# Another way to normalise the last attention block: reciprocals on the queries' partitions, four columns a tile

## Chip, cores and metric

One core of one Trainium2 chip. The time is device microseconds of one execution of the whole program; a kernel's figure is the median over several runs. The core has five engines that run their own instruction queues in order: TensorE (PE, matrix products, with weight loads listed as PEld), VectorE (DVE), ScalarE (ACT), GpSimd (POOL) and SyncE (SP, which here only issues transfers).

## What is computed

A transformer block over 2048 rows of 448 columns: layer norm, then attention with 16 heads of 28 columns, and, from the same normalised rows, a gate made by a feed-forward network. The output is the input plus attention times gate.

```python
x = A_x                                   # [1, 2048, 448], bfloat16
xn = _layernorm(x)
qkv = xn @ wqkv                           # 16 heads, 28 columns each
p = softmax(q @ k.T * 28 ** -0.5)
s = (p @ v) @ wo
g = silu(gelu(xn @ w1 + b1) @ w2 + b2)
return x + s * g
```

## The kernel before

The 16 heads lie in four groups (`G`) of four, each head padded to 32 partitions, and the 2048 queries in four chunks (`C`) of 512. A block is one group and one chunk, so there are 16 blocks. For each block the scores of 16 tiles of keys are computed in four row tiles of TensorE (line 1210), most are exponentiated on ScalarE two or three banks at a time (line 1266), some in pieces on VectorE (lines 1366 and 1417 to 1424), and the product with the values (P·V, line 1478) collects in one PSUM bank, `acc`. The values carry a column of twos, so that a head's softmax sum lies in row 28 of its 32 rows.

The last block (group 3, chunk 3) is cut by queries: one piece of 256 queries (tiles 0 and 1) and two of 128 (tiles 2 and 3); `pieces` does this. When P·V of a piece is done, `p_epi4` copies it from `acc` to `E_sb` (line 1510) and runs `p_norm4` for each of its tiles. That spreads the sums over a head's 32 partitions by a 128x128 matmul with the constant `selb` (line 1521), inverts 128x128 values on VectorE (line 1524) and multiplies (line 1527) into `qT`, which here holds the normalised attention. The 15 blocks before it do it in another way, in `p_epi`: a matmul with the four columns of `sel` brings the sums onto the queries' partitions (line 1543), VectorE inverts 16 columns (line 1546), GpSimd splits the result into a high and a low bfloat16 part (lines 1548 and 1549), and small column-tiled matmuls spread it back (line 1558).

`p_last` then multiplies a tile of the last chunk with `wo` (line 1575; groups 0 to 2 first, group 3 when the tile is normalised), and `t_oev` multiplies by the gate (line 1584), adds the input (line 1586) and issues the output transfer on SyncE's queue (line 1590). `p_out` does the same for the chunks before, with two tiles to a transfer (line 1592). The gate of the last tile is made late, behind the last exponential: a tanh on ScalarE (line 1167) and two instructions on GpSimd (lines 1169 and 1171).

The order on every engine is not written out. A planner (`run`) holds many small processes; each offers its next task with a duration, a latency and a priority, and the planner keeps a clock for each engine. It takes the task that can start first and, among those of the same engine that can start within 0.1 us of it, the one with the lowest priority number. The engines then run this fixed order, each waiting on semaphores for what it needs. When TensorE would be idle, `p_busy` fills in matmuls with zeros (line 895), until the last exponentials. Two PSUM banks that no other process holds for good go from process to process (`K.banks`); after the last scores those of the scores are added.

At the start, GpSimd makes small constants (`selb` at line 568, `bsel4` at line 571) and then the squares of a part of the key weights (line 765), while VectorE normalises the first chunk (line 696).

The lines around which all turns are these two, of the planner and of the wait for the last tile's first matmuls:

```python
near = [c for c in cand if c[1][3].E == E and c[0] <= s0 + EPS]
bank, tok = yield ("bank", lambda: K.g_done[c] and (K.on4[t] or (pre and K.exp_m >= MTOT - 7)))
```

Of the kernel before, what the change touches and what calls it, by code (L numbers as in the profile page):

```python
# [7 lines left out]
ACTF = mybir.ActivationFunctionType  # L8
ALU = mybir.AluOpType
ET = mybir.EngineType  # L10

PE, ACT, DVE, POOL, SP = ET.PE, ET.Activation, ET.DVE, ET.Pool, ET.SP
# [7 lines left out]
C = 4  # L20
# [7 lines left out]
MTOT = NBLK * T * 4  # L28
# [45 lines left out]
class _Kernel:  # L74
# [21 lines left out]
    def sb(self, name, shape, dtype=dt.bfloat16):  # L96
        return self.es.enter_context(self.nc.sbuf_tensor(name, shape, dtype))
# [160 lines left out]
    def alloc(self):  # L258
        nc = self.nc
        f32, bf = dt.float32, dt.bfloat16  # L260
        sb = self.sb
        B = _Buf
# [32 lines left out]
        self.lnv = sb("lnv", [128, T], f32)  # L295
        self.rstd = sb("rstd", [128, T], f32)
        self.nm = sb("nm", [128, T], f32)
        self.selb = sb("selb", [128, 128], bf)
        self.rc = sb("rc", [128, 16], f32)
        self.rhi = sb("rhi", [128, 16], bf)  # L300
        self.rlo = sb("rlo", [128, 16], bf)
# [8 lines left out]
        self.g_sb = self.h[:, :, 0:1792].rearrange("p c (t d) -> p c t d", d=D)  # L310
        self.osb = self.h[:, :, 1792:3584].rearrange("p c (t d) -> p c t d", d=D)
        self.iota_f = self.h[:, 1, 0:256].bitcast(f32)
        self.rf = self.w1[:, 0, 0:512].bitcast(f32).rearrange("p (a b) -> p a b", a=2)
        self.wsq = self.h[:, 1, 512:2560].rearrange("p (k n) -> p k n", k=4)
        self.stg = self.h[:, 2, 0:KT * 2 * D].rearrange("p (k w h d) -> p k w h d", k=KT, w=2, d=DH)
        ps = lambda n, s: self.es.enter_context(nc.psum_tensor(n, s, f32))
# [49 lines left out]
        self.b_P += self.b_hf[2][5:14] + self.b_hf[3][0:12] + [B() for _ in range(16)]  # L366
        self.pon = [(0, NP)]
        self.b_nm = [[B(), B()] for _ in range(C)]
        self.b_selb = B()
        self.b_E4, self.b_on4, self.b_o4 = ([B() for _ in range(4)] for _ in range(3))  # L370
        self.b_rf = [B(), B()]
        self.b_sum, self.b_sum2, self.b_m3 = B(), B(), B()
        self.b_sig3, self.b_g3 = B(), B()
        self.banks = [(self.misc[:, :], self.b_misc), (self.acc[:, :], self.b_acc)]
# [8 lines left out]
    def schedule(self):  # L383
        K = self
# [16 lines left out]
        K.g_done = [False] * C  # L401
        K.on_done = [False] * NBLK
        K.on4 = [False] * 4
        K.ln_done = 0
        K.taken = 0
        K.next_m = 0
# [85 lines left out]
    def constants(self):  # L492
        K = self
        e = self.emit

        def f(eng):
# [15 lines left out]
          writes=[K.b_pads], dur=0.1)  # L512
# [26 lines left out]
        for thr in (32.0, 64.0, 96.0):  # L539
# [3 lines left out]
              reads=[ec, tc], writes=[ec], dur=0.3)  # L543

        def f(eng):
# [6 lines left out]
          reads=[K.b_cols], writes=[tc], dur=0.3)  # L552
# [11 lines left out]
        def f(eng):  # L564
            return eng.tensor_copy(K.sel[:, :], K.ident[:, :].rearrange("p (j e) -> p j e", e=32)[:, :, DH])
        e(POOL, f, reads=[K.b_id], writes=[K.b_bsel], dur=0.2)
        selb = K.selb[:, :].rearrange("p (j e) -> p j e", e=32)
        e(POOL, lambda eng: eng.tensor_copy(selb, K.sel[:, :, None].to_broadcast([128, 4, 32])), reads=[K.b_bsel],
          writes=[K.b_selb], dur=0.3)
        bs4 = K.bsel[:, :].rearrange("p (j e) -> p e j", e=32)[:, 24:32, :]  # L570
        e(POOL, lambda eng: eng.tensor_copy(K.bsel4[:, :].rearrange("p (e j) -> p e j", j=4), bs4), reads=[K.b_bsel],
          writes=[K.b_bsel4], dur=0.2)
# [933 lines left out]
    def p_epi4(self, s):  # L1506
        K = self
        ts = ((0, 1), (2,), (3,))[s]
        sl = slice(128 * ts[0], 128 * (ts[-1] + 1))
        yield _Task(DVE, lambda eng: eng.tensor_copy(K.E_sb[:, 1, sl], K.acc[:, sl]), [K.b_acc, K.b_E[1]],  # L1510
                    [K.b_E4[t] for t in ts], 0.16 + 0.13 * len(ts), 0.0, 0)
        K.E_done = NBLK - 1 + s
        for t in ts:
            yield from K.p_norm4(t)

    def p_norm4(self, t):
        K = self
        g, c = G - 1, C - 1
        E, tE = K.E_sb[:, 1, 128 * t:128 * (t + 1)], K.b_E4[t]
        bank, tok = yield ("bank", lambda: K.g_done[C - 1])  # L1520
        yield _Task(PE, lambda eng: eng.matmul(bank[:, 0:128], K.selb[:, :], E, start=True, stop=True),
                    [tE, K.b_selb], [tok], 0.1, 0.12, 3)
        R = K.rf[:, t % 2, :]
        yield _Task(DVE, lambda eng: eng.reciprocal(R, bank[:, 0:128]), [tok], [K.b_rf[t % 2]], 0.96, 0.0, 1)
        K.banks.append((bank, tok))
        dst = K.qT[:, g, c * 512 + 128 * t:c * 512 + 128 * (t + 1)]
        yield _Task(DVE, lambda eng: eng.tensor_tensor(dst, E, R, ALU.mult), [tE, K.b_rf[t % 2], K.b_qT[g][c]],
                    [K.b_on4[t]], 0.3, 0.0, 1)
        K.on4[t] = True

    def p_epi(self, b):
# [48 lines left out]
    def t_oev(self, ps, tok, c, t):  # L1580
        K = self
        o = K.osb[:, c, t, :]
        wr = K.b_osb[c][t // 2] if c < C - 1 else K.b_o4[t]
        yield _Task(DVE, lambda eng: eng.tensor_tensor(o, ps, K.g_sb[:, c, t, :], ALU.mult),
                    [tok, K.b_g3 if (c, t) == (C - 1, 3) else K.b_g[c]], [wr], 0.63, 0.0, 3)
        yield _Task(DVE, lambda eng: eng.tensor_tensor(o, o, K.x2[:, c, t, :], ALU.add),
                    [K.b_x2[c], wr], [wr], 0.4, 0.0, 3)
        ov = K.out[0].rearrange("(c p t) d -> c p t d", p=128, t=4)[c]
        if c == C - 1:
            K.outs.append(K.dma(SP, lambda eng: eng.dma_start(ov[:, t, :], o), K.s_out[6 + t], reads=[wr]))  # L1590
        elif t % 2:
            K.outs.append(K.dma(SP, lambda eng: eng.dma_start(ov[:, t - 1:t + 1, :], K.osb[:, c, t - 1:t + 1, :]),
                                K.s_out[2 * c + t // 2], reads=[wr]))
# [10 lines left out]
    def p_last(self, t):  # L1604
        K = self
        c = C - 1
        pre = t == 3
        bank, tok = yield ("bank", lambda: K.g_done[c] and (K.on4[t] or (pre and K.exp_m >= MTOT - 7)))
        ps = bank[:, 0:D]
        yield K.t_wo(ps, tok, c, t, (0, 1, 2), 3)  # L1610
        yield ("until", lambda: K.on4[t])
        yield K.t_wo(ps, tok, c, t, (3,), 3)
        yield from K.t_oev(ps, tok, c, t)
        K.banks.append((bank, tok))
# [51 lines left out]
```

## Time and profile before

| | us |
|---|---|
| median of 4 runs (464.2 to 464.68) | 464.52 |
| the profiled execution: its time | 464.2 |
| its span | 462.4 |
| ScalarE busy | 448.4 (97%) |
| TensorE busy | 440.0 (95%) |
| VectorE busy | 372.3 (81%) |
| GpSimd busy | 37.6 (8%) |
| ScalarE: first exponential starts | 12.57 |
| ScalarE: the tanh behind the last exponential starts | 454.87 |
| reciprocal of 128x128 (line 1524), 4 times, each | 0.94 to 0.96 |
| reciprocal of 128x16 (line 1546), 15 times, each | 0.25 to 0.26 |
| output transfers of the last chunk, issue to landing, median | 1.7 |

The span runs from the first to the last recorded instruction; the time of the same execution is 1.8 us longer. Lines of a timeline give start, duration, engine, line, operation, what is written and read, how many instructions were merged, and in brackets the idle time ahead and what ended it. An engine's busy share says which engine works most on average; what an edit is worth is read in the stretch where it stands.

### The profile page before, as it was taken

Reading aid. Unit: us, or ns where it says so; the run is one execution under the profiler, and the core shown is the slowest. Engines: PE = TensorE matmul, PEld = TensorE weight load, DVE = VectorE, ACT = ScalarE, POOL = GpSimd, SP = SyncE. Lnnn points to the kernel's source line nnn. Section 1 sums busy time; section 2 is a strip of 40 time slices with the busy share of each in tenths; the row PEclk is TensorE's granted clock in tenths of the full one; section 3 lists DMA queues with packets and bytes.
Section 4 is the critical chain, followed back from the end, with each engine's and each line's share of the span. In section 5 each row is a group of like instructions: output and inputs, shape, how many; then the busy total and the mean of one; then the engine's idle time right before and its main releaser. Section 6 shows DMA issues by size and latency. Waiting matters only on the chain.

```text
span 462.4 us, 10812 instructions
## 1 busy us (share of the span) xinstructions
PE 440.0 (95%) x4555; PEld 169.8 (37%) x4555; DVE 372.3 (81%) x588; ACT 448.4 (97%) x407; POOL 37.6 (8%) x79
## 2 busy tenths in 40 slices
PE   6999999999999999999999999999999999999995
PEld 4533333333323232323233343333333344343562
DVE  8956898898879797988888844889469698888796
ACT  6999999999999999999999999999999999999994
POOL 7480000001000000100000010000000001000001
PEclk9999999999999999999999999999999999999999
DMA  8401000000000000000040000101000010100001
GB/s 264 150 2 37 2 1 0 3 1 3 2 1 1 1 1 1 2 1 2 1 140 1 1 1 0 42 2 41 0 14 28 1 41 2 42 1 21 23 23 61
DMA packets 8385, 11.17 MB, mean 24 GB/s; under 512 B 1697, under 2 KB 6993, under 8 KB 8338
## 3 DMA queue, kind: packets, MB, share of 16 engines
q1 hardware_dynamic: 8050, 9.80, 6.9%
q8 instruction: 36, 0.59, 0.5%
q10 hardware_dynamic: 288, 0.69, 0.4%
q14 instruction: 11, 0.09, 0.1%
HBM read 8.61 MB, written 1.84 MB: 23 GB/s over the span
## 4 chain that ended last, share of the span: by engine, by line
PE 52%; ACT 35%; issue 9%; DVE 2%; DMA 1%; POOL 0%; ACTq 0%; DVEq 0%; POOLq 0%
ACT P L1266 17%; PE ring L1210 14%; ACT h L1266 11%; PE acc L1478 10%; PE ring L1079 6%; ACT xnT L1266 6%; PE misc L1138 5%; PE ring L1138 4%; PE acc L895 3%; PE misc L1079 2%; PE ring L734 2%; PE misc L734 2%; PE misc L1210 1%; PE ring L1575 1%; DMA x_sb<-in_A_x_dram 1%
## 5 line engine op out<-in xcount | busy, mean ns | idle before, releaser
L1266 ACT ACTIVATE P<-ring 128x1024 bf16<-128x1024 f32 (+1 forms) x194 | 222.1, 1258 | 1.8 <-PE ring L1210 0.9
L1210 PE MATMUL ring<-qT,kT 32*128 32x512 bf16 (+2 forms) x1088 | 143.7, 358 | 12.5 <-ACT P L1266 5.2
L1266 ACT ACTIVATE h<-ring 128x1024 bf16<-128x1024 f32 (+1 forms) x97 | 114.3, 1293 | 0.2
L1210 PEld LDWEIGHTS ring<-qT,kT 32*128 32x128 bf16 x1088 | 37.1, 91 | 132.7 <-ACT P L1266 53.6
L1266 ACT ACTIVATE xnT<-ring 128x1536 bf16<-128x1536 f32 (+1 forms) x72 | 83.5, 1284 | 0.2 <-PE misc L1210 0.2
L1478 PE MATMUL acc<-P,vaug 128*32 128x512 bf16 (+2 forms) x535 | 47.5, 358 | 0.0
L895 PE MATMUL acc<-ident,zero 128*128 128x128 bf16 x525 | 41.5, 220 | 0.0
L1079 PE MATMUL ring<-xnT,w 128*128 128x512 bf16 x160 | 41.1, 381 | 0.0
L1548 POOL CAST rhi<-rc 128x16 bf16<-128x16 f32 x15 | 6.6, 440 | 389.2 <-DVE rc L1546 344.3
L895 PEld LDWEIGHTS acc<-ident,zero 128*128 128x128 bf16 x525 | 29.7, 98 | 17.6 <-issue 16.7
L1138 PE MATMUL misc<-w,h 128*128 128x448 bf16 x126 | 30.1, 355 | 0.0
L1478 PE MATMUL acc<-h,vaug 128*32 128x512 bf16 x241 | 25.1, 384 | 0.0
L1210 PE MATMUL misc<-qT,kT 32*128 32x512 bf16 (+1 forms) x64 | 24.1, 379 | 0.0
L1138 PE MATMUL ring<-w,h 128*128 128x448 bf16 x98 | 22.3, 354 | 0.1
L1366 DVE TENSOR_SCALAR x_sb<-ring 128x512 uint16<-128x512 f32 x22 | 15.2, 689 | 7.6 <-PE ring L1210 7.2
L1536 DVE CAST E_sb<-acc 128x512 bf16<-128x512 f32 x15 | 10.4, 691 | 13.2 <-PE acc L1478 13.0
L1079 PEld LDWEIGHTS ring<-xnT,w 128*128 128x128 bf16 x160 | 12.8, 97 | 18.7 <-issue 5.2
L1079 PE MATMUL misc<-xnT,w 128*128 128x512 bf16 x64 | 18.3, 383 | 0.0
L1478 PE MATMUL acc<-xnT,vaug 128*32 128x512 bf16 (+2 forms) x240 | 18.2, 330 | 0.0
L1366 DVE TENSOR_SCALAR w<-ring 128x512 uint16<-128x512 f32 x20 | 13.7, 687 | 4.0 <-PE ring L1210 4.0
L1478 PEld LDWEIGHTS acc<-P,vaug 128*32 128x32 bf16 x535 | 11.9, 95 | 13.8 <-issue 10.2
L1117 ACT ACTIVATE h<-h 128x2560 bf16<-128x2560 bf16 (+2 forms) x8 | 16.6, 2072 | 0.0
(278 smaller groups left out, 658.3 us busy)
## 6 DMA issues: line engine op xcount, KB each, us to landing
h<-in_A_x_dram SPq DMA_DIRECT2D x4, 448.0 KB, 3.1
w<-in_B_w_dram SPq DMA_DIRECT2D x1, 1568.0 KB, 7.4
w<-in_B_w_dram SPq DMA_DIRECT2D x1, 1344.0 KB, 9.0
out_dram<-h SPq DMA_DIRECT2D x6, 224.0 KB, 1.9
x_sb<-in_A_x_dram SPq DMA_DIRECT2D x2, 448.0 KB, 5.1
h<-in_A_wqkv_dram SPq DMA_DIRECT2D x3, 168.0 KB, 5.0
x_sb<-in_A_x_dram ACTq DMA_DIRECT2D x1, 448.0 KB, 4.3
out_dram<-h SPq DMA_DIRECT2D x4, 112.0 KB, 1.7
```

The lines of the kernel that those rows point to most:

```text
L734: ins = eng.matmul(bank, w[:, kt, g * 128:(g + 1) * 128], K.xnT[:, kt, c * 512:(c + 1) * 512], start=(kt == 0), stop=(kt == KT - 1))
L895: ins = eng.matmul(K.acc[:, 0:128], K.zero[:, :], K.ident[:, :], start=False, stop=True, skip_group_check=True)
L1079: ins = eng.matmul(bank, K.w1[:, kt, ft * 128:(ft + 1) * 128], K.xnT[:, kt, c * 512:(c + 1) * 512], start=(kt == 0), stop=(kt == KT - 1))
L1117: yield _Task(ACT, lambda eng, dst=dst, src=src: eng.activation(dst, src, ACTF.Gelu_apprx_tanh), rd, K.b_hf[c][f0:f0 + n] + ([K.b_h[c]] if ...
L1138: ins = eng.matmul(ps, hv[:, ft, t * 128:(t + 1) * 128], K.w2[:, ft, :], start=(ft == 0), stop=(ft == FT - 1))
L1210: return eng.matmul(dst, K.kT[32 * j:32 * j + 32, g, t * 128:(t + 1) * 128], K.qT[32 * j:32 * j + 32, g, c * 512 + q0:c * 512 + q0 + nq], ...
L1266: return eng.activation(reg[:, i0:i0 + n, :], K.ring[:, b0:b0 + n, :], ACTF.Exp, scale=SM_SCALE)
L1366: yield _Task(DVE, lambda eng: eng.tensor_scalar(K.unit[u][:, 512 * k:512 * k + 512].bitcast(dt.uint16), bank, SM_SCALE * LOG2E * 128.0, ( ...
L1478: return eng.matmul(K.acc[32 * j:32 * j + 32, q0:q0 + nq], K.vaug[:, t, 4 * g + j, :], ap[:, col:col + nq], tile_position=(0, 32 * j), sta ...
L1536: yield _Task(DVE, lambda eng: eng.tensor_copy(E, K.acc[:, :]), [K.b_acc], [tE], 0.7, 0.0, 0)
L1548: yield _Task(POOL, lambda eng: eng.tensor_copy(K.rhi[:, :], K.rc[:, :]), [K.b_rc], [K.b_rhl], 1.1, 0.0, 1)
L1575: ins = eng.matmul(ps, K.qT[:, g, c * 512 + t * 128:c * 512 + (t + 1) * 128], K.wo[:, g, :], start=(g == 0), stop=(g == G - 1))
```

## The change

The last block's tiles are normalised as the other blocks are, one tile of 128 queries at a time: a matmul with the four columns of `sel`, a reciprocal of 128x4, the split into `rhi` and `rlo`, now on VectorE instead of GpSimd, eight column-tiled matmuls, and a multiplication straight out of PSUM. All of these have priority 0. The bank is held until the multiplication is queued. The constant `selb`, the buffer `rf` and their tokens are removed. The copy of the last piece (tile 3) is made on ScalarE. In `t_oev` the gate multiplication of the last tile gets priority 2 instead of 3, and the add 3.5, 3, 2.5 and 2 for tiles 0 to 3 instead of 3. In `p_last` the first three matmuls of the last tile are offered once the selection matmul of tile 3 is queued (`K.n4 == 3`), where they were offered when few exponentials were left.

```diff
-        selb = K.selb[:, :].rearrange("p (j e) -> p j e", e=32)
-        e(POOL, lambda eng: eng.tensor_copy(selb, K.sel[:, :, None].to_broadcast([128, 4, 32])), reads=[K.b_bsel],
-          writes=[K.b_selb], dur=0.3)
...
-        yield _Task(DVE, lambda eng: eng.tensor_copy(K.E_sb[:, 1, sl], K.acc[:, sl]), [K.b_acc, K.b_E[1]],
-                    [K.b_E4[t] for t in ts], 0.16 + 0.13 * len(ts), 0.0, 0)
+        E4 = K.E_sb[:, 1, sl]
+        if s == 2:
+            yield _Task(ACT, lambda eng: eng.activation(E4, K.acc[:, sl], ACTF.Copy), [K.b_acc, K.b_E[1]],
+                        [K.b_E4[t] for t in ts], 0.3, 0.0, 0)
+        else:
+            yield _Task(DVE, lambda eng: eng.tensor_copy(E4, K.acc[:, sl]), [K.b_acc, K.b_E[1]],
+                        [K.b_E4[t] for t in ts], 0.16 + 0.13 * len(ts), 0.0, 0)
...
-        yield _Task(PE, lambda eng: eng.matmul(bank[:, 0:128], K.selb[:, :], E, start=True, stop=True),
-                    [tE, K.b_selb], [tok], 0.1, 0.12, 3)
-        R = K.rf[:, t % 2, :]
-        yield _Task(DVE, lambda eng: eng.reciprocal(R, bank[:, 0:128]), [tok], [K.b_rf[t % 2]], 0.96, 0.0, 1)
+        yield _Task(PE, lambda eng: eng.matmul(bank[:, 128:132], E, K.sel[:, :], start=True, stop=True),
+                    [tE, K.b_bsel], [tok], 0.06, 0.17, 0)
+        K.n4 = t
+        rc, hi, lo = (x[:, 4 * t:4 * t + 4] for x in (K.rc, K.rhi, K.rlo))
+        t1, t2, t3 = _Buf(), _Buf(), _Buf()
+        yield _Task(DVE, lambda eng: eng.reciprocal(rc, bank[:, 128:132]), [tok, K.b_rhl], [t1], 0.15, 0.0, 0)
+        yield _Task(DVE, lambda eng: eng.tensor_copy(hi, rc), [t1, K.b_rhl], [t2], 0.07, 0.0, 0)
+        yield _Task(DVE, lambda eng: eng.tensor_tensor(lo, rc, hi, ALU.subtract), [t1, t2, K.b_rhl], [t3], 0.07, 0.0, 0)
+
+        def f(eng):
+            ins = None
+            for k, r in enumerate((hi, lo)):
+                for j in range(4):
+                    ins = eng.matmul(bank[32 * j:32 * j + 32, 0:128], r[:, j:j + 1].to_broadcast([128, 32]),
+                                     K.ident[:, :], tile_position=(0, 32 * j), start=(k == 0), stop=(k == 1),
+                                     skip_group_check=True)
+            return ins
+        yield _Task(PE, f, [t2, t3, K.b_id], [tok], 0.12, 0.17, 0, mode="col")
+        dst = K.qT[:, g, c * 512 + 128 * t:c * 512 + 128 * (t + 1)]
+        yield _Task(DVE, lambda eng: eng.tensor_tensor(dst, bank[:, 0:128], E, ALU.mult), [tE, tok, K.b_qT[g][c]],
+                    [K.b_on4[t]], 0.3, 0.0, 0)
         K.banks.append((bank, tok))
-        dst = K.qT[:, g, c * 512 + 128 * t:c * 512 + 128 * (t + 1)]
-        yield _Task(DVE, lambda eng: eng.tensor_tensor(dst, E, R, ALU.mult), [tE, K.b_rf[t % 2], K.b_qT[g][c]],
-                    [K.b_on4[t]], 0.3, 0.0, 1)
         K.on4[t] = True
...
-                    [tok, K.b_g3 if (c, t) == (C - 1, 3) else K.b_g[c]], [wr], 0.63, 0.0, 3)
+                    [tok, K.b_g3 if (c, t) == (C - 1, 3) else K.b_g[c]], [wr], 0.63, 0.0, 2 if (c, t) == (C - 1, 3) else 3)
...
-                    [K.b_x2[c], wr], [wr], 0.4, 0.0, 3)
+                    [K.b_x2[c], wr], [wr], 0.4, 0.0, 3.5 - 0.5 * t)
...
-        bank, tok = yield ("bank", lambda: K.g_done[c] and (K.on4[t] or (pre and K.exp_m >= MTOT - 7)))
+        bank, tok = yield ("bank", lambda: K.g_done[c] and (K.on4[t] or (pre and K.n4 == 3)))
```

More of the change, by code (lines that the diff above doesn't have):

```diff
@@ L297, in alloc @@
         self.nm = sb("nm", [128, T], f32)
-        self.selb = sb("selb", [128, 128], bf)
         self.rc = sb("rc", [128, 16], f32)
@@ L312, in alloc @@
         self.iota_f = self.h[:, 1, 0:256].bitcast(f32)
-        self.rf = self.w1[:, 0, 0:512].bitcast(f32).rearrange("p (a b) -> p a b", a=2)
         self.wsq = self.h[:, 1, 512:2560].rearrange("p (k n) -> p k n", k=4)
@@ L368, in alloc @@
         self.b_nm = [[B(), B()] for _ in range(C)]
-        self.b_selb = B()
         self.b_E4, self.b_on4, self.b_o4 = ([B() for _ in range(4)] for _ in range(3))
-        self.b_rf = [B(), B()]
         self.b_sum, self.b_sum2, self.b_m3 = B(), B(), B()
@@ L403, in schedule @@
         K.on4 = [False] * 4
+        K.n4 = -1
         K.ln_done = 0
```

## The prediction

> **What bounds the kernel now.** I read the page's busy shares first (ScalarE is busy 97% of the span), then ScalarE's waits (2.2 us in all from its first exponential on), then the chain of waits, and last the timeline of the two stretches where ScalarE is not the bound: before its first exponential at 12.57 us and after its last one, behind which the tanh of line 1167 begins at 454.87 us. In between the exponentials run one after another, so the change can win only at the two ends, and can lose wherever it lets ScalarE wait. The timeline of the tail (start, duration, engine, line, operation):
>
> ```profile
> 454.87 0.69 ACT L1167 ACTIVATE w<-w 128x448 bf16<-128x448 bf16 x1
> ...
> 455.63 1.03 POOL L1169 TENSOR_TENSOR h<-w 128x448 bf16<-128x448 bf16 x1 [17.92 <-ACT w L1167]
> ...
> 455.92 0.29 DVE L1510 CAST E_sb<-acc 128x128 bf16<-128x128 f32 x1 [0.21 <-PE acc L1478]
> ...
> 456.13 0.78 DVE L1586 TENSOR_TENSOR h<-h 128x448 bf16<-128x448 bf16 x1
> ...
> 456.74 1.05 POOL L1171 TENSOR_TENSOR h<-h,w 128x448 bf16<-128x448 bf16 x1
> 456.83 0.61 DVE L1584 TENSOR_TENSOR h<-misc,h 128x448 bf16<-128x448 f32 x1
> 457.37 0.94 DVE L1524 RECIPROCAL w<-ring 128x128 f32<-128x128 f32 x1
> 458.41 0.29 DVE L1527 TENSOR_TENSOR qT<-E_sb,w 128x128 bf16<-128x128 bf16 x1
> ...
> 458.76 0.36 PE L1575 MATMUL ring<-wo,qT 128*128 128x448 bf16 x1 [1.97 <-DVE qT L1527]
> 459.16 0.62 DVE L1584 TENSOR_TENSOR h<-ring,h 128x448 bf16<-128x448 f32 x1 [0.16 <-PE ring L1575]
> 459.82 0.39 DVE L1586 TENSOR_TENSOR h<-h 128x448 bf16<-128x448 bf16 x1
> ```
>
> The reader is to see that from the end of the last copy (456.21) to the last gate multiplication (459.16) 2.95 us pass, all on VectorE's queue: an add and a multiplication of earlier tiles stand ahead of the reciprocal, and the reciprocal itself takes 0.94. From 459.16 on (multiplication, add, output transfer, span's end at 462.4) nothing is changed. Note also the add at 456.13: 0.78 us, while GpSimd runs.
>
> **Part 1, the tail.** New chain from 456.21 on. ScalarE's copy replaces VectorE's. No row has 128x128 out of PSUM on ScalarE; its 128x256 rows (line 860) take 0.38 and its 128x2 rows (line 679) 0.20, which bound it; half way in size is 0.29, VectorE's time, so I take 0, bounds -0.09 and +0.09. ScalarE's tanh is over at 455.56, nothing is queued behind the copy. Then:
> - to TensorE 0.06 (458.70 to 458.76 in the tail), the matmul with the four selection columns 0.26, to VectorE 0.04: reciprocal starts at 456.57. VectorE must be free then. Tiles 0 to 2 no longer pay 0.94 each, and have priority 0, so their multiplications and adds should be over by 455.5; that is where the 1.16 us from 456.21 to 457.37 goes.
> - reciprocal of 128x4: 128x16 takes 0.25, 128x128 0.945, that is 6.2 ns a column, so 0.17; gap 0.05: 456.79.
> - the copy to rhi and the subtraction to rlo, new on VectorE: its 128x1 rows (lines 656, 667) take 0.15 and 0.14, its 128x128 rows 0.29; near the small end, 0.15 and 0.17 with a gap of 0.05: done at 457.16.
> - eight column matmuls: the 32 of line 1558 occupy TensorE from 439.67 to 440.25, 0.018 each, the last takes 0.23; with two hops 0.06+0.15+0.23+0.05: 457.65. The three matmuls of tile 3 that now wait for n4 (0.73 us, 456.00 to 456.73 in the trace) run behind the selection matmul to about 457.2, under the VectorE chain.
> - multiplication out of PSUM 0.29 (line 1565: 0.69 for 512 columns), hop, matmul, hop 0.46: the gate multiplication starts at 458.40 instead of 459.16, **-0.76**.
>
> Now GpSimd. The two new small instructions read SBUF at 456.8 to 457.2, in the middle of line 1171. The trace shows what that can cost:
>
> ```profile
> L1586 DVE TENSOR_TENSOR h<-h x16: 380/392/777, 395.9 to 459.8; 128x448 bf16<-128x448 bf16 x16
> ```
>
> ```profile
> 6.03 0.67 DVE L696 TENSOR_SCALAR h<-x_sb,mv,rstd 128x448 bf16<-128x448 bf16 x2
> ...
> 6.85 0.29 POOL L568 COPY selb<-sel 128x128 bf16<-128x128 bf16 x1
> ...
> 7.08 0.23 POOL L571 COPY bsel<-bsel 128x32 bf16<-128x32 bf16 x1
> 7.28 0.93 POOL L765 TENSOR_TENSOR h<-h 128x448 bf16<-128x448 bf16 x1
> ...
> 7.60 1.04 DVE L696 TENSOR_SCALAR h<-x_sb,mv,rstd 128x448 bf16<-128x448 bf16 x2
> ```
>
> One add of sixteen is twice as long, the one that began 0.5 us into line 1169; it ended 0.25 us after GpSimd's instruction. The pair of line 696 takes 0.67 us at 6.03 and 1.04 at 7.60, beside line 765. So a VectorE instruction that reads SBUF behind a running two-input GpSimd instruction waits for its end. Line 1171 starts at 456.74 and takes 0.93 as line 765 does, to 457.67; the subtraction then ends at about 457.77, and the gate multiplication starts at 459.01: **-0.15**; if the copy to rhi is held as well, about 0. The two ends of this term are -0.85 (a faster ScalarE copy, no block) and 0; I take -0.15, because the nearest row, the add, was held by exactly this pair of instructions. The pair at 6.03 beside line 560 was not held, which keeps the other end alive.
>
> The Trainium skill (SBUF — State Buffer, section "Who interferes with whom") states that a VectorE instruction with two SBUF inputs contends with a GpSimd instruction that reads SBUF, and that whoever comes second blocks fully. The add at 456.13 agrees (0.78 against 0.39), and by this rule the tail is worth -0.15, without it -0.76.
>
> **Part 2, the head.** The copy that makes selb (line 568) goes. It is 0.23 us of GpSimd's queue (6.85 to 7.08), and line 765, which follows with no idle time, starts at 7.05 and ends 0.23 earlier. The held instruction at 7.60 took 0.74 where its neighbours take 0.37 to 0.39, so 0.36 of wait shrinks by 0.23. The chain of waits passes through it, then transposes, ScalarE's and VectorE's copies (ScalarE idled only 0.16 before the one at 9.21), qT and the first exponential at 12.57. Bounds -0.23 and 0 (another wait takes over); I take **-0.2**. On TensorE the column sums of line 915 may come a place earlier, 0.24 us, beside a wait.
>
> **Part 3, the middle of the last block.** Each of tiles 0 to 2 adds eight column matmuls (0.15 us) to TensorE's queue, ahead of which they wait for VectorE. Behind them stand P·V and scores. By the priorities, tile 0's group comes between the projection of the third block's last tile and P·V at 448.05:
>
> ```profile
> 448.05 0.63 PE L1478 MATMUL acc<-P,vaug 128*32 128x128 bf16 x32
> 448.61 0.40 PE L1210 MATMUL ring<-qT,kT 32*128 32x128 bf16 x12
> ```
>
> ```profile
> 449.06 2.44 ACT L1266 ACTIVATE xnT<-ring 128x1536 bf16<-128x1536 f32 x2
> ```
>
> The scores end at 449.01 and their exponential starts at 449.06: no slack. So whatever the group adds here ScalarE loses: 0.15, and up to 0.3 with a late rlo. The later scores have slack: the twelve at 450.67 feed an exponential at 451.30. Bounds 0 (dropped filler matmuls) and +0.3; I take **+0.2**.
>
> **At nothing.** The new priorities of the add (line 1586; its output transfer goes behind it on SyncE in the same order of tiles and with the same bytes): in blocks 12 to 14 each add follows its own multiplication with no other add ready; if two swap, 0.39 under 0.9 us of exponential. The bank held through the multiplication: two floating banks and, at the end, the returned score banks cover it; without them one projection, 0.7, off the path until 455. Removed buffers cost nothing.
>
> **Sum.** -0.15 - 0.2 + 0.2 = -0.15. The profiled execution took 464.2 (span 462.4 and 1.8 around it), the fastest of those shown; the median is 464.52. I forecast **464.3** for the median, 463.9 to 464.8 for this case alone.
>
> **Rivals.**
> - *No block*: GpSimd's reads are over, or fit between, when rhi and rlo come. Tail -0.76 to -0.85, head -0.2, stall 0 to 0.2: 464.52 less 0.76 to 1.05, that is 463.3 to 463.8, with the middle at 463.6. For it: the pair at 6.03; rhi is due at 456.79, near the seam at 456.66 to 456.74. Against: the add.
> - *ScalarE waits for the column matmuls*: TensorE's queue is in order, and at tiles 0, 1 and 2 it stands until rlo is written. If VectorE has a gate multiplication (0.62) ahead of the reciprocal, the wait per tile is 0.62+0.17+0.15+0.17 = 1.11, less a projection on TensorE meanwhile (0.48) and some 0.2 of slack: 0.43, three times 1.3, less 0.35 at the two ends: 464.52+0.95, **465.5**, slower. It decides where TensorE reaches the column matmuls more than 0.3 us before rlo on average. For it: no slack at 449.06. Against: before 451.64 and 452.89 TensorE itself waited for ScalarE, 0.37 and 0.25 us.
> - *The copy costs a table load*: the three loads in the trace take 1.28 each; the tanh behind the exponentials needed none, but no Copy runs there. 464.52+1.28-0.35 = 465.4. The Trainium skill (ScalarE: Activation LUTs, "Table sets: the hidden batching unit") says that copy is in every set; no row here shows it for this set.
>
> **Chances.** 0.2% of the median, about what a measurement of this kernel can tell from no change, is 0.93 us: faster is under 463.6, slower over 465.4. Forecast case 0.39 (faster 0.05, slower 0.02), no block 0.37 (faster 0.25), waits for column matmuls 0.21 (slower 0.20), table load 0.03 (slower). Faster 0.30, same 0.45, slower 0.25. The range takes in all of the no-block case and reaches up to the two slower rivals, of which about half is left out: 463.2 to 465.4.
>
> **What would show it.** In the changed profile: first exponential at about 12.35; a gap before the exponential near 449; VectorE idle before the last reciprocal near 456.5; rhi or rlo of 0.5 us or more, ending with line 1171 (right), or both under 0.2 (the no-block rival); the last gate multiplication near 459.0 or 458.4. A table load after 455 or idle times of ScalarE over 0.5 us between 446 and 455 would make it wrong.

## The result, and the profile after

The changed kernel takes **463.92 us** (median of 33 runs, 463.43 to 464.55) against 464.41 for the kernel before (53 runs beside it, 464.19 to 465.17). The ratio is 0.9988, 95% interval 0.9983 to 0.9992: a gain of 0.49 us or 0.11% of the median. The interval excludes 1, and the gain lies inside the 0.2% that the prediction counted as no change. The profiled execution took 463.88 us, with a span of 462.0 (before: 464.2 and 462.4).

Two profiles that differ by 0.3 us in time say little as totals, so I cut each into four stages at three events that every version has: the start of the first exponential that follows the first 24 ("25th"), the start of the tanh behind the last exponential, and the start of the last gate multiplication. All numbers are starts read from the timelines, and differences between them; the span's end is known to 0.1 us only.

| profile | first exp. | 25th exp. | from it to tanh | tanh to last gate mult. | to the span's end |
|---|---|---|---|---|---|
| before | 12.57 | 35.55 | 419.32 | 4.29 | 3.24 |
| after | 13.20 | 35.56 | 419.44 | 3.82 | 3.18 |

So in this pair of executions the tail gained 0.47 us, the middle lost 0.12, and the head, where the first exponential comes 0.63 *later*, is even by the 25th. That the head comes out even is an accident of these two executions: TensorE's clock stepped up at 7.36 us before and at 9.09 after, as the experiments on the head show. The tail of the changed kernel, from its timeline (start, duration, engine, line, operation, what is written and read, count, idle time ahead and what ended it):

```profile
455.00 0.61 ACT L1161 ACTIVATE w<-w 128x448 bf16<-128x448 bf16 x1
...
455.69 1.09 POOL L1163 TENSOR_TENSOR h<-w 128x448 bf16<-128x448 bf16 x1 [17.96 <-ACT w L1161]
...
455.89 0.28 ACT L1506 ACTIVATE E_sb<-acc 128x128 bf16<-128x128 f32 x1 [0.28 <-PE acc L1472]
...
456.44 0.18 DVE L1525 RECIPROCAL rc<-misc 128x4 f32<-128x4 f32 x1
456.65 0.17 DVE L1526 CAST rhi<-rc 128x4 bf16<-128x4 f32 x1
456.85 1.06 POOL L1165 TENSOR_TENSOR h<-h,w 128x448 bf16<-128x448 bf16 x1
456.86 0.16 DVE L1527 TENSOR_TENSOR rlo<-rc,rhi 128x4 bf16<-128x4 f32 x1
456.94 1.23 DVE L1599 TENSOR_TENSOR h<-h 128x448 bf16<-128x448 bf16 x1
...
457.22 0.24 PE L1533 MATMUL misc<-ident,rlo 128*32 128x128 bf16 x4
458.09 0.28 DVE L1539 TENSOR_TENSOR qT<-misc,E_sb 128x128 bf16<-128x128 f32 x1
...
458.42 0.36 PE L1588 MATMUL ring<-wo,qT 128*128 128x448 bf16 x1 [0.96 <-DVE qT L1539]
458.82 0.62 DVE L1597 TENSOR_TENSOR h<-ring,h 128x448 bf16<-128x448 f32 x1 [0.46 <-PE ring L1588]
459.48 0.39 DVE L1599 TENSOR_TENSOR h<-h 128x448 bf16<-128x448 bf16 x1
```

Read it from the bottom. The last gate multiplication (458.82) waits for its matmul, that for the multiplication into `qT` at 458.09. The column matmuls that this one needs are over at 457.46. It started 0.63 later because VectorE was not free: the add of tile 2 at 456.94, line 1599, took 1.23 us where the next add of the same shape (459.48) takes 0.39. It ran beside GpSimd's second gate instruction (line 1165, 456.85 to 457.91) and ended 0.26 after it. `rlo` at 456.86, only 0.16 long, was not held. VectorE and GpSimd met within some 0.01 us; the experiments on the tail show that which instruction is held changes from one execution to the next.

The middle, from ScalarE's timeline (an exponential of 128x1024 begins at 448.17; the line shows the next one, which waits for its scores, merged with its successor):

```profile
449.19 2.36 ACT L1260 ACTIVATE xnT<-ring 128x1536 bf16<-128x1536 f32 x2
```

and from TensorE's:

```profile
448.12 0.24 PE L1533 MATMUL ring<-ident,rlo 128*32 128x128 bf16 x4
448.18 0.63 PE L1472 MATMUL acc<-P,vaug 128*32 128x128 bf16 x32
448.74 0.40 PE L1204 MATMUL ring<-qT,kT 32*128 32x128 bf16 x12
```

The column matmuls of tile 0, eight from 448.06 on (the last four are shown), stand ahead of P·V. The scores start at 448.74 instead of 448.61, and their exponential at 449.19 instead of 449.06. From there to the tanh everything is 0.13 later (455.00 against 454.87).

The head, by ScalarE's timeline; before:

```profile
12.57 1.02 ACT L1266 ACTIVATE P<-ring 128x1024 bf16<-128x1024 f32 x1 [0.47 <-PE ring L1210]
13.49 0.29 ACT L677 ACTIVATE lnv<-mv,epsc 128x2 f32<-128x2 f32 x1
...
20.75 14.92 ACT L1266 ACTIVATE P<-ring 128x1024 bf16<-128x1024 f32 x16 [0.30 <-PE ring L1210]
35.55 1.04 ACT L1266 ACTIVATE h<-ring 128x1024 bf16<-128x1024 f32 x1
```

and after:

```profile
12.77 0.29 ACT L671 ACTIVATE lnv<-mv,epsc 128x2 f32<-128x2 f32 x1 [0.51 <-DVE mv L645]
13.09 0.20 ACT L673 ACTIVATE rstd<-lnv 128x2 f32<-128x2 f32 x1
13.20 8.38 ACT L1260 ACTIVATE P<-ring 128x1024 bf16<-128x1024 f32 x9
21.78 13.90 ACT L1260 ACTIVATE P<-ring 128x1024 bf16<-128x1024 f32 x15 [0.21 <-PE acc L1472]
35.56 1.04 ACT L1260 ACTIVATE h<-ring 128x1024 bf16<-128x1024 f32 x1
```

The two small statistics of line 671 and 673 (677 and 679 before) now stand ahead of the first exponential, not behind it. That is the greater part of why it takes 22.36 us from the first to the 25th exponential, not 22.98. The edit touches none of these lines. On TensorE the column sums (line 909, before 915) now stand ahead of the first projection of Q, and the projections of K are dealt out among those of Q. This is a different start order: with the 0.3 us of the removed `selb` copy gone from its GpSimd clock, the planner decided otherwise for other engines (e13 below changes that number alone and gets this order).

### The profile page after: what moved, and what is told of

Read it like the earlier page. It is cut to its first block, busy times and chain, and to the rows that moved or that the text cites. A ratio compares the mean times of both kernels' runs of the same rounds, so it can differ in the third digit from the quotient of the medians.

```text
span 462.0 us, 10870 instructions
## 1 busy us (share of the span) xinstructions
PE 441.0 (95%) x4578; PEld 170.7 (37%) x4578; DVE 370.3 (80%) x595; ACT 448.7 (97%) x408; POOL 37.6 (8%) x78
## 4 chain that ended last, share of the span: by engine, by line
PE 53%; ACT 35%; issue 9%; DVE 1%; POOL 1%; POOLq 0%; ACTq 0%; DVEq 0%
ACT P L1260 17%; PE ring L1204 14%; ACT h L1260 11%; PE acc L1472 10%; ACT xnT L1260 6%; PE ring L1073 6%; PE misc L1132 5%; PE ring L1132 4%; PE acc L889 3%; PE misc L1073 2%; PE ring L728 2%; PE misc L728 1%; PE misc L1204 1%; PE acc L871 1%; PE misc L1588 1%
```

## The experiments

Eleven kernels, in three sets, each timed in five rounds beside the kernel before (its median in the sets: 464.36, 464.43 and 464.41). Line numbers below are each kernel's own. The diffs show the lines on which an experiment turns, compared with the changed kernel; e13 is compared with the kernel before, and e9 and e11, which are built on e3, show only what they add to it.

The profiles in the same four stages:

| profile | first exp. | 25th exp. | from it to tanh | tanh to last gate mult. | to the span's end |
|---|---|---|---|---|---|
| e1_copy_kept | 12.54 | 35.53 | 419.41 | 4.39 | 3.17 |
| e5_old_order | 12.66 | 35.64 | 419.42 | 4.21 | 3.23 |
| e6_new_order_copy | 13.11 | 35.47 | 419.44 | 4.21 | 3.18 |
| e2_add_behind | 13.21 | 35.56 | 419.43 | 3.33 | 3.18 |
| e3_gate_dve | 12.72 | 35.08 | 419.42 | 3.38 | 3.22 |
| e7_second_later | 13.04 | 35.40 | 419.43 | 3.32 | 3.25 |
| e8_rlo_later | 12.74 | 35.10 | 419.43 | 4.21 | 3.16 |
| e9_gate_copy_dve | 13.32 | 35.68 | 419.42 | 3.56 | 3.24 |
| e11_col_behind | 12.70 | 35.06 | 419.37 | 3.39 | 3.18 |
| e12_old_start_tile3 | 13.36 | 35.72 | 419.43 | 4.43 | 3.22 |
| e13_before_new_order | 12.87 | 35.23 | 419.31 | 4.29 | 3.17 |

### The head: the removed copy, or the order that follows from it

**e1_copy_kept** keeps the copy on GpSimd, into a buffer that nobody reads; the start order is then the old one.

```diff
+        jb = K.junkb[:, :].rearrange("p (j e) -> p j e", e=32)
+        e(POOL, lambda eng: eng.tensor_copy(jb, K.sel[:, :, None].to_broadcast([128, 4, 32])), reads=[K.b_bsel],
+          writes=[_Buf()], dur=0.3)
```

> The changed kernel, but GpSimd's copy of 128 columns at the start (formerly selb) is kept, into a buffer that nobody reads; the planner's order of the start is then that of the kernel before. Theory A (the 0.49 us come from the tail alone): the same as the changed kernel, 463.9 within 0.1. Theory B (my term of -0.2 at the start is real): 464.1 or more, with the first exponential at 12.57 and the held line-690-type instruction (VectorE's normalising at 7.6) at 0.74 again.

**e5_old_order** leaves the copy out, but sets the planner's GpSimd clock ahead, so that the old order comes out.

```diff
+        self.tE[POOL] += 0.38
```

> The changed kernel without the copy on GpSimd, but with the planner's clock of GpSimd advanced as if it were there, so that TensorE's order at the start is that of the kernel before. If the start is worth 0.2 through the shorter hold and the changed order gives nothing: 0.2 below e1_copy_kept, first exponential at about 12.35. If the new order of the column sums is what cost the start of the changed kernel (its first exponential came at 13.20): 0.2 or more below the changed kernel, 463.7. Rival (the start doesn't reach the end, since a later wait takes it up): the same as both, 463.9.

**e6_new_order_copy** keeps the copy as e1 does, but the planner counts it at `dur=-0.08` (0.38 less than 0.3, the same 0.38 that e5 adds): the copy runs, and the order is the new one.

```diff
+        e(POOL, lambda eng: eng.tensor_copy(jb, K.sel[:, :, None].to_broadcast([128, 4, 32])), reads=[K.b_bsel],
+          writes=[_Buf()], dur=-0.08)
```

> The changed kernel with the copy of 128 columns kept on GpSimd at the start, but with the planner's clock as if it were not there: the new order of the start with the old work. With the three kernels before it this makes a square: copy kept or gone, order old or new. Theory (the new order is what the start gains): like the changed kernel, 463.9, and the 25th exponential as early as there at the same TensorE speed (35.1 to 35.6). Rival (the copy's 0.23 us on GpSimd is what counts): 464.2, like the two with the old order.

**e13_before_new_order** is the kernel before with that one number changed: the old last block and the new start order.

```diff
-          writes=[K.b_selb], dur=0.3)
+          writes=[K.b_selb], dur=-0.08)
```

> The kernel before, with the planner's clock as if the copy to selb took no time: its own last block and its own copy, but the new order of the start. Theory (the new order alone is worth about 0.3): 464.1, and the 25th exponential at 35.1 where TensorE runs its transposes at 7 to 9 us in 0.6 to 0.8, at 35.4 to 35.6 where it takes over 1.0. Rival (the order has no effect of its own): 464.4.

Measured medians, with ranges of 11 runs each and the ratio to the kernel before:

| | copy on GpSimd | no copy |
|---|---|---|
| new last block, old order | e1: 464.3 (463.82 to 464.47), 0.9996 [0.9988, 1.0005] | e5: 464.25 (463.67 to 464.73), 0.9994 [0.9985, 1.0003] |
| new last block, new order | e6: 464.02 (463.48 to 464.57), 0.9991 [0.9982, 0.9999] | the change: 463.92, 0.9988 [0.9983, 0.9992] |
| old last block, new order | e13: 464.08 (463.88 to 464.4), 0.9993 [0.9984, 1.0001] | |

What follows: taken against the kernel before of its own set, the order is worth 0.35 with the copy (e1 to e6), 0.38 without (e5 to the change) and 0.33 on the old last block (e13). The copy's own time is worth 0.05 to 0.08, which these intervals do not tell from nothing. The three estimates of the order agree, but each experiment's interval reaches some 0.4 us to either side, so the medians alone do not show it. With the order taken out, the new last block alone gives 0.06 (e1), 0.11 (e5) and 0.16 (e13 to the change).

The profiles seem to show this gain only at times: the 25th exponential starts at 35.53 to 35.64 in the profiles with the old order (before, e1, e5), and at 35.06 to 35.72 in those with the new one. The difference is made on TensorE between 7 and 9 us, where it transposes the normalised rows and fills its idle time with matmuls. After:

```profile
7.23 1.06 PE L803 MATMUL ring<-ident,h 128*128 128x128 bf16 x8
8.08 1.21 PE L871 MATMUL acc<-E_sb,ident 128*128 128x256 bf16 x5
9.12 0.61 PE L803 MATMUL ring<-ident,h 128*128 128x128 bf16 x8
```

and in e3_gate_dve, which has the same start:

```profile
7.23 0.80 PE L803 MATMUL ring<-ident,h 128*128 128x128 bf16 x8
7.86 0.71 PE L871 MATMUL acc<-E_sb,ident 128*128 128x256 bf16 x5
8.63 0.61 PE L803 MATMUL ring<-ident,h 128*128 128x128 bf16 x8
```

The second transposes start 0.49 apart, and so does the 25th exponential (35.08 and 35.56). The five filler matmuls one by one, with the shortest, the median and the longest of them in ns, after and in e3:

```profile
L871 PE MATMUL acc<-E_sb,ident x5: 354/418/418, 8.1 to 8.9; 128*128 128x256 bf16 x5
L871 PE MATMUL acc<-E_sb,ident x5: 273/273/273, 7.9 to 8.3; 128*128 128x256 bf16 x5
```

The same matmul takes 418 ns up to a certain moment and 273 behind it, and that moment is the clock's: the trace's record of the granted clock begins, at full speed, at 9.09 us after and at 7.61 in e3. (The share of 1.00 that the profile gives for the stretch from 7.0 to 9.3 us in both covers time ahead of that record.) The step lies between 6.60 and 7.64 us in before, e1, e3, e5, e8, e11 and e13, and between 8.48 and 9.43 in after, e2, e6, e7, e9 and e12. The kernels after, e2, e3 and e9 have the same start, so the moment goes with the execution, not with the program.

With an early step, the order's gain does show: 35.53 to 35.64 with the old order, 35.06 to 35.23 with the new one. From before to e13, which both keep the copy and start the second transposes at 8.79 and 8.80, it is 0.32, close to the 0.33 of the medians. From e13 to e8, both with the new order and a step at 6.6, the missing copy gives 0.13 more (35.23 to 35.10); from e1 to e5, with the old order, it gives nothing (35.53 to 35.64), but in e5 VectorE's normalising waited 0.38 for ScalarE's `rstd` instead. So the head's gain is for the most part the order's. With a late step the new order comes to 35.40 to 35.72; no profile has the old order with a late step.

### The tail: who is held

**e2_add_behind** queues the add of tile 2 only behind the last multiplication into `qT`.

```diff
+        if (c, t) == (C - 1, 2):
+            yield ("until", lambda: K.on4[3])
```

> The changed kernel, but tile 2's add may only be queued behind tile 3's normalising multiplication. Theory (the add, held by GpSimd's second instruction for 0.84 us, stands ahead of the multiplication): the multiplication starts at about 457.55 instead of 458.09, the last gate multiplication at about 458.3 instead of 458.82, and the time falls by 0.4 to 0.5, to 463.45. Rival (the multiplication waits for TensorE's column matmuls, not for VectorE's queue): the same, 463.9.

Measured: 463.5 (462.92 to 464.37, 11 runs), ratio 0.9984 [0.9975, 0.9993]. Its tail takes 3.33 us, 0.49 less than the change's, with the same start (35.56). The timeline:

```profile
456.84 1.06 POOL L1165 TENSOR_TENSOR h<-h,w 128x448 bf16<-128x448 bf16 x1
...
457.57 0.29 DVE L1539 TENSOR_TENSOR qT<-misc,E_sb 128x128 bf16<-128x128 f32 x1 [0.56 <-PE misc L1533]
457.78 0.38 DVE L1601 TENSOR_TENSOR h<-h 128x448 bf16<-128x448 bf16 x1
458.32 0.62 DVE L1597 TENSOR_TENSOR h<-ring,h 128x448 bf16<-128x448 f32 x1 [0.16 <-PE ring L1588]
```

The multiplication now starts when its matmuls are done (457.57), and reads PSUM and SBUF beside GpSimd in 0.29, not held. The add behind it starts 0.12 us ahead of the end of GpSimd's instruction and loses nothing that can be seen. So the 0.5 us of the profile were the held add's.

**e8_rlo_later** puts a memset of one column on VectorE ahead of tile 3's `rlo`, meant to let GpSimd come first.

```diff
+        if t == 3:
+            yield _Task(DVE, lambda eng: eng.memset(K.dum[:, :], 0.0), [t2], [K.b_dum], 0.01, 0.0, 0)
```

> The changed kernel with a one-column memset on VectorE ahead of tile 3's rlo, so that rlo starts about 0.1 us later. Theory (race): rlo always comes second and takes 0.8 to 1.0, the last gate multiplication comes 4.3 to 4.4 us after the tanh's start, and the time is that of the kernel before or a little less, 464.2 to 464.4. Rival (no race): the same as the changed kernel plus 0.1, 464.0.

Measured: 464.0 (463.81 to 464.52, 11 runs), ratio 0.9992 [0.9983, 1.0001], no different from the change and below the 464.2 to 464.4 that the theory gave. The hold is there, though:

```profile
456.19 0.17 DVE L1526 CAST rhi<-rc 128x4 bf16<-128x4 f32 x1
456.38 1.03 POOL L1165 TENSOR_TENSOR h<-h,w 128x448 bf16<-128x448 bf16 x1
456.40 1.03 DVE L1529 TENSOR_TENSOR rlo<-rc,rhi 128x4 bf16<-128x4 f32 x1
456.42 0.06 DVE L1528 MEMSET dum<- 128x1 f32 x1
```

The subtraction of 128x4 takes 1.03 instead of 0.16; the tail takes 4.21. But `rlo` starts 0.21 behind `rhi`, as in the changed kernel (456.65 to 456.86), so the trace does not show that the memset moved it. The same loss, with no memset, stands in the profiles of e1, e5 and e6 (`rlo` 1.04, tails 4.21 to 4.39; in e1 the last matmul takes 0.55 instead of 0.36 as well, behind the fall of the granted clock to a half at 458.20). So the same last block comes out either way: the changed kernel's own profile is one where `rlo` was not held. How often that is so without a profile stays open: e8's nearly equal median and the small gains of the last block alone (0.06 to 0.16, where a won race gives 0.47 less 0.12) speak for many lost races, but 15 of the changed kernel's 33 runs lie below the fastest of e8's 11 (463.81).

**e7_second_later** puts a memset of one column on GpSimd between its two gate instructions, so that VectorE comes first.

```diff
+            yield _Task(POOL, lambda eng: eng.memset(K.tcol[:, :], 0.0), [K.b_g3], [], 0.01, 0.0, 0)
```

> The changed kernel with a one-column memset on GpSimd between the last tile's two gate instructions, so that the second starts about 0.15 us later. Theory (rlo and GpSimd's second instruction start within 0.02 us of each other, and whoever comes first holds the other): rlo now always comes first and takes 0.16, the add behind it waits for GpSimd, the last gate multiplication comes 3.9 to 4.0 us after the tanh's start; the time is narrow, 463.7, with nothing above 464.2. Rival (no race; the spread has another source): spread and median as in the changed kernel, 463.4 to 464.5.

Measured: 463.33 (462.97 to 463.68, 11 runs), ratio 0.9978 [0.9969, 0.9987], better than the expected 463.7. By the medians, an instruction *added* makes the kernel faster by 0.59:

```profile
456.66 0.10 POOL L1165 MEMSET tcol<- 128x1 f32 x1
456.68 0.16 DVE L1528 TENSOR_TENSOR rlo<-rc,rhi 128x4 bf16<-128x4 f32 x1
456.76 0.38 DVE L1600 TENSOR_TENSOR h<-h 128x448 bf16<-128x448 bf16 x1
456.84 1.20 POOL L1166 TENSOR_TENSOR h<-h,w 128x448 bf16<-128x448 bf16 x1
```

Both `rlo` and the add take their shortest times, where the expectation had the add wait, and GpSimd is the one that pays: 1.20 where its second gate instruction takes 1.03 to 1.06 elsewhere. Its result is not wanted before 458.15, so this wait costs nothing. The Trainium skill (SBUF — State Buffer, "Who interferes with whom") states that the order of issue decides who blocks; e7 on the one side and the held `rlo` of e1, e5, e6 and e8 on the other agree with it (1.20 on GpSimd, 1.03 to 1.04 on VectorE).

**e3_gate_dve** takes GpSimd out: the last tile's gate is one instruction on VectorE.

```diff
-            yield _Task(POOL, lambda eng: eng.tensor_tensor(o, sg[:, 3, :], fb[:, 3, :], ALU.mult),
-                        [K.b_sig3, K.b_fsb[c % 2]], [K.b_h[c], K.b_g3], 0.85, 0.05, 0)
-            yield _Task(POOL, lambda eng: eng.tensor_tensor(o, o, fb[:, 3, :], ALU.add),
-                        [K.b_fsb[c % 2]], [K.b_h[c], K.b_g3], 0.85, 0.05, 0)
+            yield _Task(DVE, lambda eng: eng.scalar_tensor_tensor(
+                o, sg[:, 3, :], 1.0, fb[:, 3, :], op0=ALU.add, op1=ALU.mult),
+                        [K.b_sig3, K.b_fsb[c % 2]], [K.b_h[c], K.b_g3], 0.62, 0.0, 3)
```

> The changed kernel, but the last tile's gate is made by one VectorE instruction behind the tanh instead of two on GpSimd; GpSimd is idle in the tail. Theory (GpSimd holds VectorE there): every add takes 0.39, none 0.8 or more; VectorE has 0.62 more work ahead of the reciprocal, so the multiplication starts at about 457.9, and the time falls by about 0.2, to 463.7. Rival (the add at 456.94 is long for another reason): it stays at 1.2 and the time rises by 0.2 to 0.4, the added work.

Measured: **463.05** (462.92 to 463.62, 8 runs), ratio 0.9973 [0.9963, 0.9983], the lowest median here (e11, built on it, has 463.11), ahead of both kernels and of the 463.7 that was expected.

```profile
455.15 0.63 DVE L1163 SCALAR_TENSOR_TENSOR h<-w 128x448 bf16<-128x448 bf16 x1 [0.18 <-ACT w L1161]
...
456.40 0.16 DVE L1526 TENSOR_TENSOR rlo<-rc,rhi 128x4 bf16<-128x4 f32 x1
456.48 0.62 DVE L1596 TENSOR_TENSOR h<-ring,h 128x448 bf16<-128x448 f32 x1
457.13 0.29 DVE L1538 TENSOR_TENSOR qT<-misc,E_sb 128x128 bf16<-128x128 f32 x1
```

The gate instruction costs VectorE 0.63, most of it in the time in which it would wait for the copy. No instruction of the tail is held, but the tail (3.38) is no shorter than e2's (3.33) or e7's (3.32). What e3 has over e2 by its profile is the head, 35.08 against 35.56, which has the same program in both; TensorE's clock stepped at 7.61 us in the one and at 9.11 in the other. How much of its lead in the median (0.45 over e2) is of that kind, the runs do not tell.

**e9_gate_copy_dve** is e3 with the last copy back on VectorE.

```diff
-        if s == 2:
+        if s == 3:
```

> e3_gate_dve (last gate on VectorE) with the last copy back on VectorE instead of ScalarE. My term for this edit was 0, with bounds of 0.09 either way, as long as VectorE is free at the end of P.V; here the gate instruction of 0.63 stands ahead of the copy. Theory (the copy itself costs the same, its place in VectorE's queue is what it is worth): the copy starts about 0.4 us later than on ScalarE, the reciprocal too, and the time rises by 0.2 to 0.4, to 463.3 to 463.45. Rival (no difference): 463.05.

Measured: 463.63 (463.2 to 463.95, 11 runs), ratio 0.9981 [0.9972, 0.999], 0.58 above e3 and above the 463.3 to 463.45 that was expected. By the profile the copy is as long (0.28), but starts 1.19 behind the tanh's start instead of 0.89, since it stands behind the gate instruction, and the tail takes 3.56, 0.18 more. In the profile the head is late as well (25th exponential at 35.68 against 35.08), which this edit does not touch: the clock stepped at 9.33 instead of 7.61. The 0.40 of the median that the tail leaves over may be of that kind too. So the engine of the copy is worth its place in the queue, 0.18 by the tail. With GpSimd making the gate it was not tried.

**e12_old_start_tile3** puts the old condition for tile 3's first matmuls back.

```diff
-        bank, tok = yield ("bank", lambda: K.g_done[c] and (K.on4[t] or (pre and K.n4 == 3)))
+        bank, tok = yield ("bank", lambda: K.g_done[c] and (K.on4[t] or (pre and K.exp_m >= MTOT - 7)))
```

> The changed kernel with the old condition for tile 3's first three matmuls (few exponentials left, instead of the selection matmul queued). The planner then puts tile 2's add ahead of the last reciprocal instead of behind rlo. Theory (order on VectorE against GpSimd's two instructions): the add begins while GpSimd's first instruction runs, takes about 0.6 to 0.8, the reciprocal comes 0.4 to 0.6 later, rlo falls into GpSimd's second instruction and waits for its end; the last gate multiplication comes 4.3 to 4.5 us after the tanh's start and the time is 464.1 to 464.4. Rival (the place of these matmuls doesn't matter): 463.9, as the changed kernel.

Measured: 464.54 (463.95 to 464.82, 11 runs), ratio 0.9998 [0.999, 1.0007]: 0.62 above the change, all that it had won, and above the 464.1 to 464.4 that was expected. By the profiles the tail takes 4.43, which is 0.61 more than the change's with its race won and 0.04 to 0.22 more than the tails with it lost, and the head is 0.16 later. Three matmuls of tile 3 stand in front of P·V, which starts 0.48 behind the tanh's start (455.63) instead of 0.21 (455.21), and then the late chain falls into GpSimd's second instruction:

```profile
457.00 1.05 POOL L1165 TENSOR_TENSOR h<-h,w 128x448 bf16<-128x448 bf16 x1
457.09 0.17 DVE L1525 RECIPROCAL rc<-misc 128x4 f32<-128x4 f32 x1
457.29 0.78 DVE L1526 CAST rhi<-rc 128x4 bf16<-128x4 f32 x1
```

The cast to `rhi`, with a single input, is held to 458.07, the end of GpSimd's instruction (458.05). The reciprocal beside the same instruction, which reads PSUM, is not (0.17).

### The middle

**e11_col_behind** is e3 with the column matmuls of tile 0 queued only behind the next scores.

```diff
+        if t == 0:
+            u0 = K.sc_u
+            yield ("until", lambda: K.sc_u > u0)
```

> e3_gate_dve (last gate on VectorE, GpSimd idle in the tail), and tile 0's eight column matmuls may only be queued behind the next scores. Theory (these matmuls are what made ScalarE wait 0.13 us before the exponential at 449.2): no gap there, the exponentials follow each other by 1.34 and 0.90, and the time is 0.13 below e3_gate_dve, 462.9. Rival (the gap is the selection matmul's or P.V's own): the gap and the time stay, 463.05.

Measured: 463.11 (462.86 to 463.53, 8 runs), ratio 0.9974 [0.9964, 0.9985]: nothing gained, a miss. The gap at that place is gone (from the exponential at 447.66 to the next 0.90, not 1.01 as in e3), but from 447.66 to the tanh it still takes 6.77 us, against 6.82 in e3 and 6.71 before. About half of the wait turns up at a later exponential: the one at 450.85 starts 0.96 behind the one before it, where e3 has 0.90. The 0.05 that is left is too little for the medians to show.

## Why the prediction stood

The total came out 0.38 below the forecast (463.92 against 464.3), just inside the range given for that case alone. The three terms have the right signs, the tail and the middle by the two profiles, the head by the medians and by the profiles with an early clock step. Step by step:

- **Tail, -0.15 (bounds -0.85 and 0).** The mechanism was right: beside GpSimd's second gate instruction VectorE's instructions from SBUF are held until it ends, at 457.91 in the profile after (forecast 457.67). The forecast gave that instruction 0.93, as line 765 takes, where the prediction's own lines show 1.05 for it; with 1.05 its sum would have been -0.03. The size was one value for what is a meeting within 0.01 us: -0.47 in the profile after, with the add held instead of `rlo`; -0.08 where `rlo` is held (e5, e6, e8; +0.10 in e1, with its slow last matmul). The forecast lies between. The profile fits neither of its two pictures: `rhi` and `rlo` are both under 0.2, as the no-block rival said, and yet the gate multiplication starts at 458.82, not at 458.4, because the step left out what VectorE has queued *behind* `rlo`, the add of tile 2. Without any hold, the chain from the end of the last copy to the gate multiplication was worked out as 2.19; e2 shows 2.16 (456.16 to 458.32). The small terms: reciprocal 0.17 forecast and 0.18 measured, `rhi` 0.15 and 0.17, `rlo` 0.17 and 0.16.
- **ScalarE's copy, 0 (±0.09).** Its length was right, 0.28 against 0.29. That VectorE's queue ahead of the copy would also count was left out; in e9 this place is worth 0.18.
- **Head, -0.2.** The size was near (0.33 to 0.38 for the order and 0.05 to 0.08 for the copy, by medians), but the step that failed is this one: it took the gain to be the 0.23 us by which line 765 ends earlier. That hold did shrink (the pair of line 690 ends at 8.39 instead of 8.64), yet e1 to e5, which removes just this, gives 0.05 by the medians, and e13 to e8 gives 0.13 by profiles with an early clock step. Most of the gain comes with the planner's new order, 0.32 to 0.38. The prediction saw a corner of that order ("the column sums of line 915 may come a place earlier") and put it at nothing beside a wait. It forecast the first exponential at 12.35; it came at 13.20, behind the two statistics that the order put ahead of it and behind the late clock step (12.70 to 12.74 in e3, e8 and e11, with the same order and an early step). So the right size was partly luck.
- **Middle, +0.2 (bounds 0 and +0.3).** Right mechanism and place: the exponential near 449 is late by 0.13, and nothing else between there and the tanh. By the stages it is +0.09 to +0.12 in every kernel with the new last block, except e11 (+0.05).
- **At nothing.** The priorities of the add and of the gate multiplication: put back, they give the same program, instruction for instruction, so they do nothing. The condition `K.n4 == 3` was counted within the tail, where its three matmuls run under VectorE's chain (456.26 to 456.99 in the profile after), and had no price of its own; e12 puts it at 0.62 by the median, of which the tail shows at most 0.61.
- **The rivals.** No table load: the tanh is at 455.00, the copy 0.28 at 455.89, and nothing lies between. ScalarE does not wait for the column matmuls of tiles 1 and 2: one idle time of 0.13, not three of 0.43. The no-block rival is what e2, e3 and e7 made true, at 463.05 to 463.5, where it was put at 463.3 to 463.8 (463.47 to 463.76 by its own terms).

What stays open: how often the changed kernel wins its race when no profile is taken, and what the order is worth when TensorE's clock steps late, which moves the head by 0.3 to 0.7 us between profiles of programs that begin alike.

## What to carry to other kernels

Where an instruction of one engine can hold one of another, price a short instruction by whom it meets and by what is queued behind it, not by its own length: here a 0.16 us subtraction cost up to 1.04, and one more 0.1 us instruction on the other engine bought 0.59. If the result of the slower engine is not needed at once, let it come second, or take its work away. And where a planner makes the order, a duration that is changed in one corner moves others far from it: change the number alone, as e13 did, before the gain is put down to the work that was removed. Before two profiles are compared in their first microseconds, look in both for the moment at which the matmuls become shorter: here it differed by up to 2.8 us and hid a gain of 0.3.

## What the runs showed of the hardware that was not expected

- A meeting within 0.02 us decides 0.87 us of an instruction and some 0.4 of the tail (3.82 against 4.21): `rlo` starting 0.01 behind GpSimd's instruction took 0.16 (after, e2), and 0.00 to 0.02 behind it 1.03 to 1.04 (e1, e5, e6, e8). The starts in the trace do not resolve who came first.
- A cast of 128x4 with one input from SBUF is held as well as a subtraction with two (e12, 0.78 against 0.17); a reciprocal or a multiplication that takes one input from PSUM is not (0.17, 0.29).
- The moment at which TensorE's clock steps up changes from one execution to the next: 6.60 to 9.43 us from the span's start in the 13 profiles, with the first matmul at 3.85 or 3.86 in all of them. A filler matmul of 128x256 takes 0.42 ahead of it and 0.27 behind it. The Trainium skill (TensorE: Matmul & The Clock Gate, "Part 1: The HAM clock gate (the "warmup" mystery)") says that the change to full clock depends on a free-running window of about 3.4 us and so on the run. The traces agree: the moments spread over 2.83 us, less than one such window, and the stretch at full clock is 450.56 or 453.97 us long in every profile, 3.41 apart.
